# A new order of all pieces, and pad instructions ahead, in an attention and maxout-FFN kernel on one core

## The chip, the cores and the metric

One NeuronCore of a Trainium2 chip runs the whole program. The metric is device time in microseconds (us) of one execution, as a median over runs. Engines by the profile's names: PE is TensorE's matmul, PEld its weight load, DVE is VectorE, ACT is ScalarE, POOL is GpSimd, SP is SyncE.

## The reference

Eight batches of eight heads, 576 rows, head dimension 64, 32 memory slots; then a maxout feed-forward layer over all 4608 rows.

```python
def _attn_ref(q, k, v, phi):
    a = softmax(phi, axis=2)                       # over the sequence
    k_m = np.einsum('bhsm,bhsd->bhmd', a, k)
    v_m = np.einsum('bhsm,bhsd->bhmd', a, v)
    scores = (1/np.sqrt(64)) * np.matmul(q, k_m.transpose(0, 1, 3, 2))
    attn = softmax(scores, axis=-1)                # over the 32 slots
    return np.matmul(attn, v_m)

def _moe_ref(x, w1, w2, w3, w_out):                # x: 4608 x 512
    h = np.maximum(np.maximum(x @ w1, x @ w2), x @ w3)
    return h @ w_out                               # d_ff = 768
```

(The softmaxes are written out in the reference with maximum, exp and sum; they are shortened here.)

## The kernel before

The kernel never forms the attention output. Per batch it folds v_m into the weights, so that the feed-forward layer is applied to the attention weights themselves (256 of them per row instead of 512 columns). It uses max(a, b, c) = c + max(a - c, b - c, 0): w1 - w3 and w2 - w3 replace w1 and w2, and w3 goes with w_out into one small product.

The work is a list of pieces, written out by hand in one string (lines 810 to 838). A word such as `F8@2!` means piece F8 of batch 2; the mark ! swaps the engine that does the piece's copy or elementwise work. `issue` (line 769) calls the function of each letter, and every engine's instruction stream is the order of the list: nothing is rearranged afterwards. An engine takes its instructions in that order and stops at the first one whose inputs aren't ready. The letters:

- L0 to L3, J, H, h: loads of phi, k, v, q of a batch (J, H, h are parts), all issued by POOL except phi of batch 0 (SP); Y: the weights. q, k, v and the weights are turned from fp32 into bf16 on the way.
- E: exp of phi (ACT). B: the products with k and v (72 small matmuls, line 256), which from batch 2 on read a packed copy of k that r0 makes (POOL, or ACT with !). N: normalisation; K: transposes of the result (line 315); Q: transposes of q (DVE, line 330).
- S: scores and their exp (lines 351, 360). a, s, c, m, X: softmax by transposes on DVE (lines 410 to 450), m on POOL or, with !, on DVE. M, R and, in batches 0 and 1, part of X do it with ones-matmuls.
- W, O: products of w3 and w_out (lines 189, 197). V: w1 - w3 and w2 - w3 in four column ranges, on DVE or, with !, on POOL (line 218). In batch 0 the folds use w1, w2, w3 as they come, and V overwrites w1, w2 after that.
- D0 to D2 (and D4 in batch 0): the folded weights of a batch by columns, D3: the small product (line 462).
- F0 to F11: the hidden layer, even for the first operand, whose relu goes to ACT or, with !, DVE; odd for the second, whose max is always on DVE (line 526).
- t, T: the output product of batches 0 and 1 (lines 672, 690, 699, 708), where t is its first four matmuls; T4@7 is the last (lines 742, 753). U, A, P: the output product of batches 2 to 7 in Strassen-Winograd form: sums of weights (U, on POOL or DVE), of hidden rows (A), seven products (P, line 624).
- g: sends an output tile of batch 0 (ACT's queue, line 730). Other outputs are sent by SP.
- Z: matmuls on zeros in the first 20 us.

Results of PE lie in PSUM, eight banks that the digits of `banks` deal out in the order of the pieces; a digit is the bank, or the first of two. A piece can't start on a bank before the copy of the piece that had it is done. The output tile `ot` has four buffers, taken in turn:

```python
opool = ctx.enter_context(tc.tile_pool(name="opool", bufs=4))
...
ot = opool.tile([P, 2, DM], FP32, name="ot")[:, 0]
```

The four outputs of batch 0 stay in them until their g; T3@1 and T4@1 take the first two again. Inputs phi and q have two buffers each, k as loaded two, v and the packed k three.

Of the kernel before, what the change touches and what calls it, by code (L numbers as in the profile page):

```python
# [9 lines left out]
BF16 = mybir.dt.bfloat16  # L10
# [5 lines left out]
def kernel(  # L16
# [12 lines left out]
    nc = tc.nc  # L29

    B, H, S, D = q.shape
    M = phi.shape[-1]
    P = 128
# [11 lines left out]
    const = ctx.enter_context(tc.tile_pool(name="const", bufs=1))  # L45
# [18 lines left out]
    K1 = NP * NC * KS  # L64
# [20 lines left out]
    def load_ph(b):  # L85
        ph = inp.tile([P, NP, NC, M], FP32, name="ph", tag="ph")
        loaded.setdefault(b, {})["ph"] = ph
        dst = ph.rearrange("p j c m -> p j (c m)")
        if b == 0:
            for h in halves:  # L90
                nc.sync.dma_start(out=dst[:, h], in_=by_pair(phi, b)[:, h])
        else:
            nc.gpsimd.dma_start(out=dst, in_=by_pair(phi, b))

    def load_kv(b, i, h=slice(0, NP)):
        kv = vs[b % 3] if i else ks[b % 2]
        nc.gpsimd.dma_start(  # L97
            out=kv[:, h].rearrange("p j c d -> p j (c d)"),
            in_=by_pair((k, v)[i], b)[:, h],
        )  # L100

    def pack(b, swap):
        out_, in_ = krs[b % 3][:, :, :, 0:D], ks[b % 2]
        if swap:
            nc.scalar.copy(out=out_, in_=in_)
        else:
            nc.gpsimd.tensor_copy(out=out_, in_=in_)  # L107

    def load_q(b, h=slice(0, NP)):
        if "q" not in loaded.setdefault(b, {}):  # L110
            loaded[b]["q"] = inp.tile([P, NP, NC, D], BF16, name="qq", tag="qq")
        nc.gpsimd.dma_start(  # L112
            out=loaded[b]["q"][:, h].rearrange("p j c d -> p j (c d)"),
            in_=by_pair(q, b)[:, h],
        )

    def load_w(i):
        w = (moe_w1, moe_w2, moe_w3)[i]
        nc.gpsimd.dma_start(  # L119
            out=w_sb[:, :, i], in_=w.rearrange("(j p) f -> p j f", p=P)  # L120
        )
# [3 lines left out]
    def load_wo():  # L125
        nc.gpsimd.dma_start(out=wo_sb, in_=moe_w_out.rearrange("(t p) c -> p t c", p=P))
# [3 lines left out]
    warm = const.tile([P, BANK], BF16, name="warm")  # L130
# [7 lines left out]
    for i in range(P // M):  # L138
# [4 lines left out]
    banks = iter(  # L143
        "".join(
            """
            00232204420145545045026406426402640264023462467420742602462062460264024603604206
            42604620642164646240624607402604260240402402420724062042642024204204260424026427
            402742002442072420426045026520026265260602406243352
            """.split()
        )  # L150
    )
# [1 line left out]
    def one_bank():  # L153
        return psum[:, int(next(banks))]
# [5 lines left out]
    def warm_up(n):  # L160

        po = one_bank()
        for _ in range(n):
            nc.tensor.matmul(  # L164
                po[:, 0:BANK], lhsT=warm[:, 0:P], rhs=warm, start=True, stop=True
            )
# [46 lines left out]
    def w_diff(n, swap):  # L213

        c, end = [(0, BANK), (BANK, DF), (2 * BANK, 2 * DF), (DF, 2 * BANK)][n]
        while c < end:
            e = min(end, (c // DF + 1) * DF)
            (nc.gpsimd if swap else nc.vector).tensor_tensor(  # L218
                out=w12[:, :, c:e],
                in0=w12[:, :, c:e],  # L220
                in1=w_sb[:, :, 2, c % DF : c % DF + e - c],
                op=ALU.subtract,
            )
            c = e
# [202 lines left out]
    def att_rec(b, g):  # L427
        x = st[b]["ts"][:, groups(g)]
        nc.vector.reciprocal(out=x, in_=x)  # L429
# [302 lines left out]
    def ffn2_last(b, c0):  # L732
# [18 lines left out]
        for i, (c, po) in enumerate(zip(cs, pos)):  # L751
# [13 lines left out]
            else:  # L765
                nc.scalar.copy(out=ot[:, c], in_=po)
                nc.scalar.dma_start(out=rows, in_=ot[:, c])

    def issue(b, n, swap):

        i = int(n[1:]) if len(n) > 1 else None
        {
            "I": lambda: [make_identity(nc, ident)]
            + [nc.gpsimd.memset(x[:, :, :, D:], 1.0) for x in krs],
            "Y": lambda: load_w(i) if i < 3 else load_wo(),
            "L": lambda: load_ph(b) if i == 0 else load_q(b) if i == 3 else load_kv(b, i - 1),
            "J": lambda: load_q(b, halves[i]),
            "H": lambda: load_kv(b, i % 2, halves[i // 2]),
            "h": lambda: load_kv(b, 0, slice(i, i + 1)),
            "r": lambda: pack(b, swap),  # L780
            "E": lambda: [att_exp(b, h) for h in (halves if b == 0 else [slice(0, NP)])],
            "B": lambda: att_kv(b, i),
            "N": lambda: att_kv_norm(b, swap, i),
            "K": lambda: att_kv_t(b, swap, i),
            "Q": lambda: att_q(b, i),
            "S": lambda: att_score(b),
            "a": lambda: att_t(b, i),
            "s": lambda: att_sum(b, i),
            "c": lambda: att_rec(b, i),
            "m": lambda: att_mul(b, i, swap),  # L790
            "X": lambda: (ones_mul if (b, i) in ONES else att_back)(b, i),
            "M": lambda: ones_sum(b, i),
            "R": lambda: ones_rec(b, i),
            "D": lambda: fold(b, i, swap),
            "F": lambda: ffn1(b, i, swap),
            "T": lambda: ffn2(b, i, swap),
            "U": lambda: combine_w(b, i, swap),
            "A": lambda: combine_a(b, i, not swap),
            "P": lambda: products(b, i, swap),
            "W": lambda: w3_t(i, swap),  # L800
            "g": lambda: send(i),
            "d": lambda: fold_begin(i),
            "t": lambda: ffn2_begin(b, i),
            "O": lambda: w3_o(i, swap),
            "V": lambda: w_diff(i, swap),
            "Z": lambda: warm_up(i),
        }[n[0]]()


    for w in """  # L810
        E@0 h2@0 h3@0 h0@0 h1@0 L3@0 Z25@0 B0@0 Y2@0 I@0 N0@0 Z2@0 K0@0! Q0@0 Q1@0 Z9@0 S@0 Z2@0
        M0@0 M1@0 R0@0 R1@0 W0@0 Y3@0 W1@0 W2@0 Z6@0 O1@0 H3@0 O3@0 O2@0 H1@0 X1@0 B1@0
        X0@0 N1@0 K1@0 O0@0 Y0@0 D1@0! D0@0! D3@0 F10@0 F0@0! F8@0 Y1@0 L0@1 L1@1 J0@1
        F2@0! F6@0 V0@0! D4@0! D2@0 E@1 J1@1 F4@0! F1@0 F5@0 L2@1 F3@0 F7@0 F9@0 L3@2
        F11@0 B0@1 N0@1! t1@0 L1@2 t2@0 Q1@1 Q0@1 T2@0 K0@1! V1@0 V3@0 T1@0 S@1 L0@2
        B1@1 U0@9! N1@1! M1@1 a0@1 R1@1 t3@0 K1@1! T3@0 L2@2 s0@1 L1@3 c0@1 V2@0 D0@1
        D1@1! L0@3 D2@1 L2@3 t0@0 r0@2 X1@1 m0@1! X0@1 T0@0 F10@1! Q0@2 F6@1 E@2 F7@1
        F0@1 g2@0 F11@1 L3@3 F1@1 D3@1 Q1@2 F2@1 B@2 U1@9 F4@1 L1@4 L0@4 N@2 F3@1 F8@1
        K@2 g1@0 F5@1 L2@4 S@2 F9@1 D1@2! t3@1 E@3 D0@2 D2@2 D3@2 L3@4 a@2 T3@1 s@2 U3@9
        T4@1! c@2 m@2! r0@3 X@2 B@3 F0@2 U0@2 N@3 F8@2! F6@2 K@3 U1@2 Q0@3 L1@5 F2@2  # L820
        L0@5 Q1@3 U3@2 F10@2 g0@0 F3@2 F4@2 F9@2 F11@2 U2@9 S@3 a@3 s@3 t2@1 c@3 g3@0
        D3@3 D2@3 L2@5 U2@2 D0@3 U0@3 t0@1 r0@4! E@4 F1@2 T0@1! U1@3 F5@2 T2@1! F7@2
        t1@1 m@3 L3@5 A0@2! X@3 L0@6 T1@1! F6@3 F4@3! D1@3! B@4 N@4 L1@6 A1@2! F0@3 Q1@4
        F2@3 Q0@4 L2@6 A2@2! F8@3 K@4! F7@3 P1@2! F1@3 S@4 P2@2 F10@3 D0@4 a@4 D1@4!
        P0@2 A3@2! s@4 c@4 F3@3 P4@2 E@5 r0@5! F11@3 F9@3 m@4 F5@3 L3@6 P5@2 A0@3! T4@3!
        A1@3! D3@4 B@5 X@4 N@5 D2@4 Q1@5 Q0@5 P6@2 F2@4 K@5 P3@2 F10@4! S@5 L1@7 P1@3!
        D2@5 D1@5! a@5 F11@4 P2@3 F8@4 s@5 c@5 U2@3 L0@7 F4@4! F0@4 F6@4 r0@6! L2@7 P0@3
        F1@4 F7@4 F9@4 P4@3 E@6 A2@3! A3@3! F3@4 F5@4 P3@3 D0@5 m@5 L3@7 U3@3 D3@5 B@6
        A0@4! A1@4! X@5 N@6 P5@3 F6@5 F8@5! Q0@6 r0@7 F2@5 Q1@6 F10@5 K@6! F9@5 U0@5
        F4@5 F7@5 P6@3! S@6 E@7 F3@5 P1@4 a@6 F5@5 F11@5 P2@4 D0@6 U0@4 B@7 D3@6 U2@4  # L830
        N@7 s@6 P0@4 A2@4! F0@5 F1@5 Q1@7 K@7! U1@4 A3@4! P4@4 D1@6! A0@5! D1@7! c@6
        D2@7! m@6 P3@4! U3@4 P5@4! D0@7 D2@6 D3@7 U2@6 Q0@7 X@6 T4@5 S@7 A1@5! A3@5!
        P6@4! F10@6 a@7 F6@6 s@7 F4@6 F11@6 F0@6 F7@6 c@7 P1@5 P2@5 F2@6! U2@5 F5@6 F3@6
        P0@5 U1@5 F1@6 m@7 F8@6 A2@5! X@7 P4@5 P3@5 F4@7 U0@6 U1@6 F10@7 U3@5 F9@6 P5@5!
        F5@7 F8@7 A0@6! P1@6! A1@6! F2@7 F6@7 F0@7 P6@5! U0@7 F7@7 F3@7 F1@7 P2@6! F11@7
        F9@7 A0@7 P0@6 A2@6! A1@7 P4@6 A3@6 U3@6! P1@7 P2@7 A2@7 P5@6 P3@6 U2@7! U1@7
        P4@7 P0@7! A3@7 P6@6 U3@7! P5@7 P3@7! P6@7! T4@7!
    """.split():
        n, b = w.rstrip("!").split("@")
        issue(int(b), n, w.endswith("!"))  # L840


# [28 lines left out]
```

## Time and profile before

| | |
|---|---|
| time, median of 3 runs | 160.61 us (160.39 to 161.18) |
| the profiled execution | 160.76 us, of which the span is 159.0 us |
| busy in the span: PE | 149.6 us (94%), 2218 matmuls |
| PEld | 100.3 us (63%) |
| DVE | 116.8 us (73%) |
| ACT | 98.8 us (62%) |
| POOL | 109.2 us (69%) |
| granted TensorE clock | 0.999 |
| DMA queues, share of 16 engines' span | POOL's 70.2%, the two others for data 15.8% and 2.2% |

The span is the profiled time between the first and the last event of the execution; the rest of the 160.76 us lies around it. Times within the profile are counted from the span's start. A line of the timeline reads: start, duration, engine, line of the kernel, operation, output <- input, shapes, count, and in brackets the idle time before it and what ended it. A line of the windows by stage reads: the stretch and its length, then busy time and number of instructions of PE, PEld, DVE, ACT and POOL, granted clock, DMA share and GB/s. A line of the waits reads: engine, line and output, <- whom it waited for: us in total, times, longest.

### The profile page before, as it was taken

Reading aid. Unit: us, or ns where it says so; the run is one execution under the profiler, and the core shown is the slowest. Engines: PE = TensorE matmul, PEld = TensorE weight load, DVE = VectorE, ACT = ScalarE, POOL = GpSimd, SP = SyncE. Lnnn points to the kernel's source line nnn. Section 1 sums busy time; section 2 is a strip of 40 time slices with the busy share of each in tenths; the row PEclk is TensorE's granted clock in tenths of the full one; section 3 lists DMA queues with packets and bytes.
Section 4 is the critical chain, followed back from the end, with each engine's and each line's share of the span. In section 5 each row is a group of like instructions: output and inputs, shape, how many; then the busy total and the mean of one; then the engine's idle time right before and its main releaser. Section 6 shows DMA issues by size and latency. Waiting matters only on the chain.

```text
span 159.0 us, 5179 instructions
## 1 busy us (share of the span) xinstructions
PE 149.6 (94%) x2218; PEld 100.3 (63%) x2228; DVE 116.8 (73%) x203; ACT 98.8 (62%) x142; POOL 109.2 (69%) x101
## 2 busy tenths in 40 slices
PE   6987798999798999999999999999999999999992
PEld 2442443574456538556776768887774888888871
DVE  2022803698988899787989688999998895679871
ACT  3205335723888699799699878886788826424110
POOL 7961102995039948889999999799969997890000
PEclk9999999999999999999999999999999999999999
DMA  5999999999999999999999999999303500332554
GB/s 150 168 199 209 205 210 211 281 207 210 207 281 225 298 236 243 307 262 214 323 246 277 213 255 284 278 239 246 111 0 136 200 4 0 132 132 70 177 187 164
DMA packets 22934, 31.78 MB, mean 200 GB/s; under 512 B 1152, under 2 KB 18560, under 8 KB 22912
## 3 DMA queue, kind: packets, MB, share of 16 engines
q0 software_dynamic: 16128, 21.43, 70.2%
q1 hardware_dynamic: 6064, 8.85, 15.8%
q10 hardware_dynamic: 720, 1.18, 2.2%
q8 instruction: 17, 0.28, 0.7%
q14 instruction: 5, 0.04, 0.1%
HBM read 39.32 MB, written 9.44 MB: 307 GB/s over the span
## 4 chain that ended last, share of the span: by engine, by line
PE 72%; DMA 19%; POOL 5%; issue 1%; ACT 1%; POOLq 0%
PE psum L513 26%; PE psum L624 24%; DMA w_sb<-in_moe_w_dram 13%; DMA kvr<-in_v_dram 6%; PE psum L462 5%; PE psum L690 4%; PE psum L672 3%; PE psum L256 3%; PE psum L699 2%; PE psum L351 2%; POOL ko L97 1%; PE psum L708 1%; POOL qq L112 1%; POOL w_sb L119 1%; PE psum L753 1%
## 5 line engine op out<-in xcount | busy, mean ns | idle before, releaser
L513 PE MATMUL psum<-hx,wp 128*128 128x288 bf16 x384 | 53.7, 286 | 0.7 <-DVE wp L181 0.3
L513 PEld LDWEIGHTS <-wp 128*128 128x128 bf16 x384 | 36.6, 98 | 12.3 <-issue 1.5
L526 DVE TENSOR_TENSOR hx<-psum,h 128x576 bf16<-128x576 f32 x48 | 34.1, 744 | 3.3 <-PE psum L513 2.7
L177 ACT CAST wp<-psum 128x1024 bf16<-128x1024 f32 (+1 forms) x30 | 28.2, 993 | 2.7 <-PE psum L462 2.3
L175 ACT ACTIVATE h<-psum 128x576 bf16<-128x576 f32 x38 | 23.8, 651 | 8.9 <-PE psum L513 8.7
L624 PEld LDWEIGHTS <-hx 128*128 128x128 bf16 x192 | 18.4, 98 | 3.5 <-issue 0.9
L360 ACT ACTIVATE e<-psum 128x576 bf16<-128x576 f32 x16 | 9.5, 649 | 7.5 <-PE psum L351 7.5
L549 POOL TENSOR_TENSOR w_sb<-hx 128x1024 bf16<-128x1024 bf16 x5 | 10.6, 2130 | 4.0 <-DVE hx L526 2.6
L164 PE MATMUL psum<-warm 128*128 128x512 bf16 x42 | 11.8, 435 | 1.4 <-DVE warm L131 1.2
L330 DVE STREAM_TRANSPOSE qT<-qq 128x576 f32<-128x576 f32 x16 | 11.6, 757 | 2.0 <-DMA qq<-in_q_dram 2.0
L624 PEld LDWEIGHTS <-w_sb 128*128 128x128 bf16 x120 | 11.4, 98 | 2.5 <-issue 0.7
L107 POOL COPY kvr<-ko 128x2304 bf16<-128x2304 bf16 x3 | 6.3, 2108 | 7.7 <-DMA ko<-in_k_dram 7.7
L218 POOL TENSOR_TENSOR w_sb<-w_sb 128x2048 bf16<-128x2048 bf16 x1 | 4.1, 4065 | 10.4 <-PE psum L462 10.4
L436 POOL TENSOR_TENSOR t<-t,sm 128x1152 bf16<-128x1152 bf16 x5 | 10.6, 2127 | 0.6 <-DVE sm L429 0.5
L549 POOL TENSOR_TENSOR w_sb<-w_sb,hx 128x1024 bf16<-128x1024 bf16 x5 | 10.6, 2128 | 0.3
L234 ACT ACTIVATE e<-ph 128x1152 bf16<-128x1152 f32 (+1 forms) x9 | 9.6, 1063 | 1.8 <-DMA ph<-in_phi_dram 1.8
L549 POOL TENSOR_TENSOR hx<-hx 128x1024 bf16<-128x1024 bf16 x5 | 10.7, 2130 | 0.0
L549 POOL TENSOR_TENSOR twb<-wp 128x256 bf16<-128x256 bf16 x11 | 7.3, 670 | 3.9 <-ACT wp L177 3.9
L624 PE MATMUL psum<-w3T,hx 128*128 128x256 bf16 x72 | 9.8, 273 | 0.0
L624 PE MATMUL psum<-wo_sb,hx 128*128 128x256 bf16 x72 | 9.8, 273 | 0.0
L656 DVE TENSOR_TENSOR ot<-psum,snap 128x512 f32<-128x512 f32 x12 | 8.3, 689 | 1.9 <-PE psum L624 1.3
L97 POOL DMA_DIRECT2D ko<-in_k_dram x11 | 7.7, 700 | 2.9 <-DMA qq<-in_q_dram 1.5
(106 smaller groups left out, 272.2 us busy)
## 6 DMA issues: line engine op xcount, KB each, us to landing
out_dram<-ot SPq DMA_DIRECT2D x8, 512.0 KB, 4.2
qq<-in_q_dram POOLq DMA_DIRECT2D x7, 576.0 KB, 13.5
ph<-in_phi_dram POOLq DMA_DIRECT2D x7, 576.0 KB, 15.3
ko<-in_k_dram POOLq DMA_DIRECT2D x7, 576.0 KB, 16.1
kvr<-in_v_dram POOLq DMA_DIRECT2D x7, 576.0 KB, 18.0
out_dram<-ot SPq DMA_DIRECT2D x14, 256.0 KB, 2.2
w_sb<-in_moe_w_dram POOLq DMA_DIRECT2D x3, 768.0 KB, 17.9
out_dram<-ot ACTq DMA_DIRECT2D x4, 256.0 KB, 6.2
```

The source lines that it names most:

```text
L97: nc.gpsimd.dma_start(out=kv[:, h].rearrange("p j c d -> p j (c d)"), in_=by_pair((k, v)[i], b)[:, h],)
L164: nc.tensor.matmul(po[:, 0:BANK], lhsT=warm[:, 0:P], rhs=warm, start=True, stop=True)
L175: nc.scalar.activation(out=out_, in_=in_, func=AF.Relu)
L177: nc.scalar.copy(out=out_, in_=in_)
L234: nc.scalar.activation(out=s["e"][:, js], in_=loaded[b]["ph"][:, js], func=AF.Exp)
L330: nc.vector.transpose(out=s["qT"][:, j].rearrange("p j c r e -> p (j c r e)").bitcast(FP32), in_=loaded[b]["q"][:, j].rearrange("p j c d - ...
L360: nc.scalar.activation(out=e2[:, a].rearrange("p (t r c) -> p t r c", t=2, c=NC), in_=sc[a][:, :, 0:SH].rearrange("p t (c r) -> p t r c", ...
L436: (nc.vector if swap else nc.gpsimd).tensor_tensor(out=t, in0=t, in1=x.to_broadcast(list(t.shape)), op=ALU.mult,)
L513: nc.tensor.matmul(acc[:, h, 0:SH], lhsT=wps[b][:, g, w * DF + ft * P : w * DF + (ft + 1) * P], rhs=attn[:, g, c0 : c0 + SH], start=(g == ...
L526: nc.vector.tensor_tensor(out=hT[:, row(ft), (b % 2) * S : (b % 2 + 1) * S].rearrange("p (h n) -> p h n", h=2), in0=a, in1=s["h1", ft], op ...
L549: eng.tensor_tensor(out=out_, in0=in0, in1=in1, op=op)
L624: nc.tensor.matmul(po[:, q * CH : (q + 1) * CH], lhsT=lhs(k, q), rhs=rhs(k), start=(i < 3 and k == 0 and q == 0), stop=(k == KT and q == 1 ...
```

## The change

The list of pieces gets another order and, for 62 pieces, the other setting of the mark !; the set of pieces is the same. Up to F10@0 the order is as before. The banks are dealt out anew to fit. q of batch 2 (L3@2) is issued after k and v of that batch (L1@2, L2@2), not before. A new piece p makes n copies of a single column of the zero tile `warm` into a tile of two columns that nobody reads: 41 on DVE (p41@0!, first in the list), 8, 30 and 14 on ACT around E@0 and after K0@0. The diff, with the order cut after batch 3's first pieces:

```diff
+    pads = const.tile([P, 2], BF16, name="pads")
+
+    def pad(n, swap):
+
+        for i in range(n):
+            (nc.vector.tensor_copy if swap else nc.scalar.copy)(
+                out=pads[:, swap : swap + 1], in_=warm[:, 0:1]
+            )
...
+            "p": lambda: pad(i, int(swap)),
...
-        E@0 h2@0 h3@0 h0@0 h1@0 L3@0 Z25@0 B0@0 Y2@0 I@0 N0@0 Z2@0 K0@0! Q0@0 Q1@0 Z9@0 S@0 Z2@0
+        p41@0! p8@0 E@0 p30@0 h2@0 h3@0 h0@0 h1@0 L3@0 Z25@0 B0@0 Y2@0 I@0 N0@0 Z2@0 K0@0! p14@0 Q0@0 Q1@0 Z9@0 S@0 Z2@0
         M0@0 M1@0 R0@0 R1@0 W0@0 Y3@0 W1@0 W2@0 Z6@0 O1@0 H3@0 O3@0 O2@0 H1@0 X1@0 B1@0
-        X0@0 N1@0 K1@0 O0@0 Y0@0 D1@0! D0@0! D3@0 F10@0 F0@0! F8@0 Y1@0 L0@1 L1@1 J0@1
-        F2@0! F6@0 V0@0! D4@0! D2@0 E@1 J1@1 F4@0! F1@0 F5@0 L2@1 F3@0 F7@0 F9@0 L3@2
-        F11@0 B0@1 N0@1! t1@0 L1@2 t2@0 Q1@1 Q0@1 T2@0 K0@1! V1@0 V3@0 T1@0 S@1 L0@2
-        B1@1 U0@9! N1@1! M1@1 a0@1 R1@1 t3@0 K1@1! T3@0 L2@2 s0@1 L1@3 c0@1 V2@0 D0@1
-        D1@1! L0@3 D2@1 L2@3 t0@0 r0@2 X1@1 m0@1! X0@1 T0@0 F10@1! Q0@2 F6@1 E@2 F7@1
-        F0@1 g2@0 F11@1 L3@3 F1@1 D3@1 Q1@2 F2@1 B@2 U1@9 F4@1 L1@4 L0@4 N@2 F3@1 F8@1
-        K@2 g1@0 F5@1 L2@4 S@2 F9@1 D1@2! t3@1 E@3 D0@2 D2@2 D3@2 L3@4 a@2 T3@1 s@2 U3@9
-        T4@1! c@2 m@2! r0@3 X@2 B@3 F0@2 U0@2 N@3 F8@2! F6@2 K@3 U1@2 Q0@3 L1@5 F2@2
-        L0@5 Q1@3 U3@2 F10@2 g0@0 F3@2 F4@2 F9@2 F11@2 U2@9 S@3 a@3 s@3 t2@1 c@3 g3@0
+        X0@0 N1@0 K1@0 O0@0 Y0@0 D1@0! D0@0! D3@0 F10@0 F8@0 F0@0 F6@0! F4@0 Y1@0 D2@0!
+        D4@0 L0@1 L1@1 J1@1 F2@0 F1@0 F11@0 F3@0 F7@0 V1@0! F5@0 F9@0 E@1 B0@1 N0@1!
+        t0@0 t2@0 J0@1 Q1@1 t1@0 L2@1 Q0@1 K0@1! V2@0 L0@2 T2@0! S@1 V0@0 T1@0 a0@1 U0@9
+        B1@1 M1@1 V3@0! s0@1 N1@1! t3@0 c0@1 m0@1! K1@1 R1@1 T0@0! D1@1! X0@1 X1@1 D0@1!
+        T3@0! D2@1 E@2 F8@1! L1@2 F2@1! L2@2 F6@1 F3@1 L3@2 r0@2 F4@1 F5@1 D3@1 B@2 N@2!
+        F7@1 F10@1 Q0@2 F0@1 K@2! Q1@2 F9@1 F11@1 S@2 F1@1 D1@2! D2@2 t3@1 g2@0 g1@0
+        L1@3 a@2 U1@9 s@2 L0@3 L2@3 c@2 m@2! L3@3 L1@4 E@3 D3@2 D0@2 X@2 L0@4 T3@1 r0@3
+        T4@1 B@3 F10@2 F2@2 N@3 U2@2 F11@2 g0@0 F6@2 U0@2 F3@2 K@3! U1@2 F4@2 Q0@3 F0@2
+        U2@9 L2@4 Q1@3 L3@4 F8@2 g3@0 F5@2 F9@2 S@3 L0@5 L1@5 t2@1 L2@5 a@3 D0@3 D2@3
...
```

The swapped pieces that the prediction speaks of further on are r0@7 (from POOL to ACT) and A2@6 (from POOL to DVE).

More of the change, by code (lines that the diff above doesn't have):

```diff
@@ L145 @@
             """
-            00232204420145545045026406426402640264023462467420742602462062460264024603604206
-            42604620642164646240624607402604260240402402420724062042642024204204260424026427
-            402742002442072420426045026520026265260602406243352
+            00232204420145545045026402640640260426016724247642042604260426042604620461246042
+            60420642046214642640246042672406420462024024002460264026306463460460603464063460
+            264026404646020460260360404304640404026426436367372
             """.split()
@@ L821 @@
-        L0@5 Q1@3 U3@2 F10@2 g0@0 F3@2 F4@2 F9@2 F11@2 U2@9 S@3 a@3 s@3 t2@1 c@3 g3@0
[L822 to L837, printed above, removed]
+        X0@0 N1@0 K1@0 O0@0 Y0@0 D1@0! D0@0! D3@0 F10@0 F8@0 F0@0 F6@0! F4@0 Y1@0 D2@0!
@@ new lines @@
+        T4@1 B@3 F10@2 F2@2 N@3 U2@2 F11@2 g0@0 F6@2 U0@2 F3@2 K@3! U1@2 F4@2 Q0@3 F0@2
+        U2@9 L2@4 Q1@3 L3@4 F8@2 g3@0 F5@2 F9@2 S@3 L0@5 L1@5 t2@1 L2@5 a@3 D0@3 D2@3
+        r0@4! D3@3 E@4 s@3 U3@9 c@3 t1@1 m@3 F1@2 T1@1 F7@2 T2@1 L3@5 t0@1 A0@2! X@3
+        T0@1 F6@3! F7@3 F2@3 D1@3! L0@6 B@4 A2@2! N@4 F4@3 Q1@4 F0@3 F10@3 U3@2 A1@2!
+        F5@3 F8@3 Q0@4 K@4 P1@2 F9@3 S@4 L1@6 P2@2! a@4 D1@4! s@4 D0@4 A3@2! c@4 F1@3
+        m@4 U0@3 P4@2 F3@3 E@5 r0@5! P0@2 F11@3 U1@3 X@4 P5@2 T4@3! D3@4 B@5 D2@4 N@5
@@ new lines @@
+        L2@6 P6@2 F0@4 Q0@5 Q1@5 F8@4 K@5 P3@2! S@5 F6@4! F4@4 F2@4 a@5 F7@4 D2@5 D1@5!
+        s@5 F10@4 c@5 L3@6 P1@3 F3@4 E@6 P2@3! F9@4 r0@6! A0@3! F11@4 A1@3! F1@4 P4@3
+        L0@7 F5@4 A3@3! U2@3 P0@3 D0@5 B@6 m@5 X@5 L1@7 D3@5 A2@3! N@6 Q0@6 P3@3 F6@5
+        F0@5 Q1@6 A0@4! F4@5! P5@3 F10@5 F8@5! L2@7 K@6! F2@5! F5@5 U3@3 E@7 P6@3! S@6
+        F7@5 r0@7! a@6 P1@4 L3@7 F11@5 U2@4 U0@5 F9@5 A1@4! F1@5 U0@4 P2@4! D0@6 B@7
+        U1@4 A3@4! A2@4! U3@4 N@7! D3@6 s@6 P0@4! F3@5 K@7! P4@4 U2@5 c@6 D1@6! D2@7!
@@ new lines @@
+        Q1@7 D1@7! P3@4 P5@4 D2@6 Q0@7 D3@7! D0@7 T4@5! U0@6 S@7 P6@4 m@6 X@6 a@7 A0@5!
+        A1@5! F6@6 F8@6! U1@5 s@7 P1@5 F10@6 c@7 F2@6 P2@5! A2@5! m@7 F9@6 F11@6 F0@6
+        A3@5! P4@5! F1@6 F7@6 P0@5 U3@5 X@7 F4@6 F5@6 F3@6 P5@5 F8@7 F2@7 P3@5! F4@7
+        F5@7 A0@6! U1@6 U0@7 P6@5 A1@6! U2@6 F0@7! F6@7! F10@7 F1@7 F11@7 P1@6! F3@7
+        F9@7 U2@7 P2@6 F7@7 A2@6 P4@6 A3@6 U1@7 A0@7 U3@6! P0@6 A1@7 P1@7 P5@6 P3@6 P2@7
+        A2@7 A3@7 P4@7 P6@6 U3@7! P0@7 P5@7! P3@7! P6@7! T4@7!
```

## Prediction

> **What bounds it now.** I read the page first, then windows by stage, TensorE's (PE) timeline from 25 to 62 us, the queues' landings, and the waits.
>
> ```profile
> 0.00:25.00 25.00, 20.85 (x268) 9.85 (x272) 6.80 (x23) 8.60 (x13) 10.63 (x23) 1.00 1.07 191
> 25.00:60.00 35.00, 33.10 (x624) 18.58 (x627) 29.12 (x46) 24.70 (x39) 21.82 (x19) 1.00 1.18 240
> 60.00:150.00 90.00, 89.79 (x1294) 67.25 (x1288) 76.84 (x129) 64.50 (x90) 76.75 (x59) 1.00 0.76 187
> 150.00:159.00 9.00, 5.89 (x55) 4.58 (x53) 3.99 (x7) 1.01 (x3) 0.00 (x0) 0.99 0.56 193
> ```
>
> The windows (first column after the length: PE busy) say where a new order can act. From 60 to 150 us PE lacks 0.21 of 90 us. Both orders hold the same pieces, so PE's work there is the same, and only a new stall can change that stage. The end is 12 products and T4 back to back, then a store. The first 25 us keep their order. What is left is 25 to 60, where PE lacks 1.9 us, and the timeline shows some of it:
>
> ```profile
> 27.21 0.66 PE L513 MATMUL psum<-hx,wp 128*128 128x288 bf16 x4
> 28.17 2.13 PE L513 MATMUL psum<-hx,wp 128*128 128x288 bf16 x16 [0.30 <-DVE wp L181]
> ...
> 49.73 0.65 PE L513 MATMUL psum<-hx,wp 128*128 128x288 bf16 x4 [0.23 <-DVE hx L526]
> 50.59 0.80 PE L256 MATMUL psum<-kvr,e 64*32 64x130 bf16 x72 [0.21 <-ACT wp L177]
> ...
> 53.67 0.48 PE L351 MATMUL psum<-qT,kvt 32*32 32x288 bf16 x32
> ```
>
> ```profile
> PE psum L256 <- DMA kvr<-in_v_dram: 0.8, 1, 0.8
> ```
>
> F10 to F0 of batch 0 start 0.96 apart where an F piece takes 0.49; B1@1 waits 0.77 for v of batch 1. The last fence is a line of the waits between 25 and 62 us. Loads bound this stage as much as PE: asked issue by issue, POOL's queue lands in order of issue, v1 at 40.53 (31.68 + 8.85), then q2 43.43, k2 46.27, ph2 47.82, v2 50.46, k3 54.09, ph3 55.64, v3 59.08. So q takes 2.90, k 2.84, ph 1.55, v 2.64.
>
> **The change, step by step.** The sum goes against the profiled run's own 160.76 us (span 159.0 and 1.76 around it), 0.15 over the median 160.61.
>
> *Batch 0's first products (27 to 35 us).* F8 now comes before F0, and F8's columns are D1's, which ScalarE (ACT) has copied at 27.15. F10, F8, F0 run at 27.2, 27.7, 28.2: the 0.47 hole closes. F6 and F4 follow to 29.65. D2 needs w2, which lands at 30.04 (8.77 + 21.28) in either order: 0.4 given back. D4 ends near 30.8, then seven F of 0.49 with 0.05 of wait for D4's copy: B0@1 starts near 34.4 (before: 34.93; k1 lands at 34.26).
>
> *V on POOL.* V0, 4.07 us and behind a wait of 10.4, becomes V1 and V3, 2.1 each by half the columns, and U0@9, 1.65. Behind V1 in POOL's queue stand J0@1 and the loads after it: J0@1 issues near 28.6 instead of 30.95, V3 runs to 34.6, then k2, v2, q2 by 36.9. The queue is still working off earlier issues until 36.28, so no load becomes late or early by this: v1 lands at 40.53 again. VectorE (DVE) gives up V1, V3 and U0@9 (0.6 each) and takes V0 (1.16).
>
> *Up to B1@1.* t0 (0.87) is now done before it. B0@1 34.4, t0 35.1, t2, t1, K0, T2, S@1 38.9, T1 end at 40.2; B1@1 waits for v1 as before, 40.58. The gain there is t0's 0.87. T3, T0, D0 to D2 of batch 1 then run without the old gaps but wait for copies; I get the first F of batch 1 at 45.4 against 46.06: 0.66 ahead.
>
> *q of batch 2 behind v.* With the durations above: ph2 42.1, k2 44.9, v2 47.6, q2 50.46. B@2 needs POOL's copy of k (44.9 + 2.1 = 47.0) and v2. It starts near 48.8 with six F done (before 50.59 with seven): 1.3 ahead. Q0@2 now waits for q2 at 50.46, and the F copies of DVE queue behind it: Q0, Q1 end at 52.15, S@2 starts at 52.3 against 53.67, both with 11 F done. So 1.37 ahead.
>
> *The stores g2 and g1.* Here the gain goes. The output tile has four buffers; T3@1 and T4@1 take those of T2@0 and T1@0, so they wait until g2 and g1 have landed. Before, ACT issued these at 48.2 and 53.0. Now both stand on ACT behind the copies of D1@2 and D2@2, that is, behind S@2.
>
> ```profile
> L730 ACTq DMA_DIRECT2D out_dram<-ot x4: 338/338/374, 48.2 to 65.7; - x4
> DMA to landing us min/median/max: 5.8/6.2/6.5
> ```
>
> ```profile
> 59.99 1.13 ACT L177 COPY ot<-psum 128x512 f32<-128x512 f32 x2
> ```
>
> The first fence is the answer for the stores' line, the second ACT's timeline. g1 landed at 53.01 + 5.82 = 58.83, 1.6 before T4@1's copy at 60.47. From S@2's start in the new order: first exp done 1.25 (0.58 to its start, 0.65, as at 53.67), D1 and D2 on PE 0.6, issue of g2 and g1 0.4, landing 6.2, T4@1's copy (now DVE) 0.75: 9.2. F11@2, the third F of batch 2, takes the banks of T3@1 and T4@1, so it starts at 52.3 + 9.2 = 61.5. Without the wait it would be 60.35 (t3, D3, D0, T3 and T4 at their old lengths put B@3 at 58.55, then B 0.8 and two F). The third F of batch 2 started at 61.35 before (60.38 + 2 x 0.49). Equal PE work, 0.15 later. N@3 on DVE stands behind T4@1's wait and K@3, F3@2 behind N@3; I get S@3 at 65.7 with ten F done against 65.04 with nine, 0.17 late. v3 lands at 57.5 to 59.1 (without the two stores that shared 53 to 59, or as before), so B@3 is not the last wait.
>
> *POOL's queue past r0@2.* r0@2 now stands ahead of batch 3's loads. POOL waits there for k2 (44.9), packs to 47.0, issues k3 (before: 36.0), spends 1.65 on U1@9, then issues ph3 and v3 at 49.5 and 50.2. The queue works on q2 until 50.46 and the quickest load in the trace landed 4.0 after its issue (the first k, 1.25 to 5.22), so k3 can land at 53.3 and v3 isn't held. Were v3 late by 2.5 us or more, B@3 would be the last wait instead of the stores.
>
> *The rest of the order, from 65 us.* By pieces times the rows' durations, from S@3 on DVE and POOL keep their load within 0.5 us (A2@6 goes from POOL, 2.1, to DVE, 0.6) and ACT gains 1.9 (r0@7, 2.1). In 60 to 150 these engines are idle for 13, 25 and 13 us, and the least distance between a bank's copy and its next use is about 0.9 us of PE work in both orders. Cost 0; without that cover, a single held copy is 0.3 to 0.6.
>
> *Pads.* 41 on DVE, 8, 30 and 14 on ACT; no instruction so small stands in the trace. Bounds: 0.01 (the one-column MEMSETs, 3 in 0.08 us) and 0.25 (ACT's 128-column COPY). I take 0.14: two 576-column exps start 0.54 apart, 1024-column CASTs 0.90, which leaves 0.08 fixed, and the 1152-column exp from SBUF adds 0.06. Their cover is in ACT's and DVE's waits:
>
> ```profile
> 3.71 0.68 ACT L234 ACTIVATE e<-ph 128x576 bf16<-128x576 f32 x1 [1.68 <-DMA ph<-in_phi_dram]
> 10.71 0.37 ACT L177 COPY kvt<-psum 128x256 bf16<-128x256 bf16 x1 [5.47 <-PE psum L315]
> 13.56 1.19 ACT L360 ACTIVATE e<-psum 128x576 bf16<-128x576 f32 x2 [2.47 <-PE psum L351]
> 9.52 0.17 DVE L276 RECIPROCAL rden<-psum 128x2 f32<-128x2 f32 x1 [7.61 <-PE psum L256]
> ```
>
> 8, 30, 14 and 41 times 0.14 are 1.1, 4.2, 2.0 and 5.7: all fit, cost 0. What the pads are to avoid I don't find: ACT's three CASTs from 57.29 and DVE's copies near 50 run without a gap that PE doesn't explain. Gain 0. [...]
>
> Sum: 160.76 + 0.15 = 160.91 for a profiled run, 160.8 as a median.
>
> **Rivals.**
> *The head start survives.* If g1 lands within 5.0 us, T4@1's copy isn't held, F11@2 starts at 60.35, 1.0 earlier than the third F before: 159.6. For it: stores in the last 12 us of the span land in 2.2. Against: those have the queues to themselves, while the four of ACT needed 5.8 to 6.5 with POOL's loads running, which they still do near 55. [...] Chance 0.25, also for other gains there.
> *Slower: head start lost, hold kept.* Decided at S@2. If Q0@2's wait for q2 or a late copy puts S@2 where it was, 53.67, the 9.2 us behind it put F11@2 at 62.87, 1.5 late: 162.1. For it: one late copy anywhere in 27 to 52 is enough, and q2 is now the last load. Against: v2 and k2 are 2.9 and 1.4 earlier. 0.16.
> *Pads overrun.* At 0.25 each, 52 pads leave ACT about 3.3 late at S@0's exp, of which 1.35 of waits absorb: 2 us, 162.7. 0.05.
> *The order does nothing*: 160.6, 0.04.
>
> **The numbers.** The hold, 0.50, has its own range from 160.4 (q2-bound S@2 at 52.1) to 161.9. About 0.10 of it is over 0.8 late. 0.5%, 0.8 us, is about what a measurement of this kernel tells from no change. Faster 0.25; same 0.40 + 0.04 = 0.44; slower 0.10 + 0.16 + 0.05 = 0.31. The range 159.4 to 162.1 leaves out little of the first rival and the far side of the others.
>
> **What would show it.** Right: g2 and g1 issued on ACT near 54.2, landing near 60.5; PE idle over 1 us before the third F of batch 2, put down to a DVE or ACT copy of ot; B1@1 still at 40.6; S@2 near 52.3. Wrong: no such gap, or S@2 not earlier; pads ending after 10.7 on ACT; PE idle past 65 us, which I have at none.

## The result, and the profile after

The changed kernel takes 165.57 us (median of 4 runs, 165.16 to 167.69) against 160.53 us: a ratio of 1.030, 95% interval 1.0265 to 1.0334. It is slower, by 5.0 us. (The run of 167.69 had a lower clock, 0.969; such runs count in the medians but not in the ratios, here and below.) The profiled execution is one of 165.16 us, with a span of 163.0 (before: 160.76 and 159.0). So 4.0 us were lost inside the span and 0.4 outside it.

The windows by stage, with the columns explained with the profile before, answer to the four lines shown there:

```profile
0.00:25.00 25.00, 21.55 (x255) 10.83 (x257) 12.89 (x62) 18.02 (x65) 10.63 (x23) 0.93 1.07 189
25.00:60.00 35.00, 33.79 (x679) 19.03 (x670) 27.98 (x41) 26.37 (x44) 21.63 (x20) 1.00 1.16 224
60.00:150.00 90.00, 87.34 (x1242) 64.17 (x1230) 74.53 (x121) 64.04 (x90) 75.15 (x60) 0.98 0.80 190
150.00:163.00 13.00, 9.97 (x93) 8.25 (x90) 6.95 (x13) 2.71 (x5) 0.00 (x0) 0.99 0.47 161
```

From 25 to 60 us the new order is denser, as meant: 33.79 us of PE against 33.10. But the first 25 us ran at a granted clock of 0.93 instead of 1.00, and the stretch from 60 to 150, where PE lacked 0.21 us before, now lacks 2.66 and has a clock of 0.98. PE's timeline, from 28 to 67 us, shows where:

```profile
28.40 2.62 PE L513 MATMUL psum<-hx,wp 128*128 128x288 bf16 x20
...
41.55 0.75 PE L256 MATMUL psum<-kvr,e 64*32 64x64 bf16 x72
...
49.51 0.83 PE L256 MATMUL psum<-kvr,e 64*32 64x130 bf16 x72
...
53.21 0.49 PE L351 MATMUL psum<-qT,kvt 32*32 32x288 bf16 x32
...
60.13 1.15 PE L513 MATMUL psum<-hx,wp 128*128 128x288 bf16 x8
62.31 0.28 PE L513 MATMUL psum<-hx,wp 128*128 128x288 bf16 x1 [1.02 <-ACT ot L177]
64.00 2.80 PE L513 MATMUL psum<-hx,wp 128*128 128x288 bf16 x11 [1.41 <-DVE ot L181]
```

The holes of before are closed: batch 0's first five F pieces run without a gap (28.40), and B1@1 (41.55) no longer waits for v. B@2 (49.51, with one F fewer ahead of it) and S@2 (53.21) are 1.08 and 0.46 earlier than before. Then two F of batch 2 run, and the third stands for T3@1's copy and again for T4@1's. The answer for the stores' line, and the lines of ACT and of DVE that take the two output tiles, name what those copies wait for:

```profile
L730 ACTq DMA_DIRECT2D out_dram<-ot x4: 338/356/450, 55.2 to 68.7; - x4
DMA to landing us min/median/max: 6.4/6.9/7.6
```

```profile
55.20 0.86 ACTq L730 DMA_DIRECT2D out_dram<-ot  x2
...
61.67 0.58 ACT L177 COPY ot<-psum 128x512 f32<-128x512 f32 x1 [1.89 <-DMA out_dram<-ot]
```

```profile
63.26 0.69 DVE L181 COPY ot<-psum 128x512 f32<-128x512 f32 x1 [3.29 <-DMA out_dram<-ot]
```

g2 and g1 are issued at 55.20 and 55.61 and land at 61.59 and 63.17. The third F gets its second bank at 64.00. Before, three F ran without a stop from 60.36, the third from 61.35:

```profile
60.36 1.65 PE L513 MATMUL psum<-hx,wp 128*128 128x288 bf16 x12
...
65.04 0.48 PE L351 MATMUL psum<-qT,kvt 32*32 32x288 bf16 x32
```

S@3 starts at 69.53 with ten F of batch 2 done (65.04 with nine before, so 4.0 behind after 0.49 for the piece more): all of the span's loss is there by then, and PE is full behind it in both kernels.

The lead is the other place. ACT's and DVE's timelines, and PE's, from 2 to 20 us:

```profile
5.06 6.75 ACT L774 COPY pads<-warm 128x1 bf16<-128x1 bf16 x30
11.71 0.36 ACT L177 COPY kvt<-psum 128x256 bf16<-128x256 bf16 x1
11.97 3.14 ACT L774 COPY pads<-warm 128x1 bf16<-128x1 bf16 x14
15.02 1.18 ACT L360 ACTIVATE e<-psum 128x576 bf16<-128x576 f32 x2
```

```profile
1.93 7.80 DVE L774 COPY pads<-warm 128x1 bf16<-128x1 bf16 x41
9.72 0.17 DVE L276 RECIPROCAL rden<-psum 128x2 f32<-128x2 f32 x1
```

```profile
15.71 1.18 PE L372 MATMUL psum<-e,blkones 128*128 128x288 bf16 x4 [1.60 <-ACT e L360]
16.68 2.75 PE L189 MATMUL psum<-ident,w_sb 128*128 128x128 bf16 x24
```

The same two lines of PE before:

```profile
14.26 0.94 PE L372 MATMUL psum<-e,blkones 128*128 128x288 bf16 x4 [0.23 <-ACT e L360]
15.61 1.51 PE L189 MATMUL psum<-ident,w_sb 128*128 128x128 bf16 x24 [0.40 <-DMA w_sb<-in_moe_w_dram]
```

A pad takes ACT 0.22 us (3.14 / 14) and DVE 0.19 (7.80 / 41). ACT's copy of K0 comes 1.0 later than before, its exp of S@0 1.5 later, and PE stands 1.60 for it where it stood 0.23. The W products behind it (L189) then take 2.75 us instead of 1.51. The windows ahead of that place and at it, and around the stores' wait, say why (after the length: PE, PEld, DVE, ACT, POOL busy, then the clock):

```profile
12.45:15.86 3.41, 1.77 (x38) 0.62 (x37) 0.59 (x1) 3.06 (x14) 0.16 (x1) 1.00 1.18 208
15.86:19.27 3.41, 3.39 (x28) 2.92 (x28) 1.33 (x2) 3.00 (x5) 0.70 (x1) 0.50 1.24 209
60.24:63.65 3.41, 1.33 (x9) 0.79 (x9) 0.39 (x1) 1.68 (x3) 3.33 (x5) 1.00 1.18 255
63.65:67.06 3.41, 3.06 (x15) 2.04 (x15) 2.09 (x7) 0.65 (x1) 3.41 (x5) 0.50 1.11 313
```

The granted clock fell to 0.50 from 15.86 to 19.27 us and from 63.65 to 67.06, for 3.41 us each time. The two starts lie 47.79 us apart, 14 times 3.41; from this I read windows of 3.41 us, one behind the other. In the windows just ahead PE was busy 1.77 and 1.33 us, shares of 0.52 and 0.39. The first half clock costs W 1.24; the second makes the eleven F matmuls behind the hold take 2.80, where the same eleven at full clock take 1.51 (in the run with ten pads and the hold, below).

### The profile page after: what moved, and what is told of

The parts are those of the page before. It is cut to its first block, busy times and chain, and to the rows that moved or that the text cites. A ratio compares the mean times of both kernels' runs of the same rounds, so it can differ in the third digit from the quotient of the medians.

```text
span 163.0 us, 5266 instructions
## 1 busy us (share of the span) xinstructions
PE 152.7 (94%) x2217; PEld 102.3 (63%) x2228; DVE 122.3 (75%) x236; ACT 111.1 (68%) x203; POOL 107.4 (66%) x102
## 4 chain that ended last, share of the span: by engine, by line
PE 78%; ACT 11%; DMA 7%; issue 2%; DVE 1%; SPq 0%; ACTq 0%; DVEq 0%
PE psum L513 27%; PE psum L624 23%; ACT pads L774 5%; DMA out_dram<-ot 5%; PE psum L462 5%; PE psum L672 4%; PE psum L690 4%; PE psum L197 3%; PE psum L256 3%; DMA ph<-in_phi_dram 2%; PE psum L699 2%; PE psum L351 2%; PE psum L189 2%; ACT wp L177 2%; ACT e L360 1%
## 5 line engine op out<-in xcount | busy, mean ns | idle before, releaser
L513 PE MATMUL psum<-hx,wp 128*128 128x288 bf16 x384 | 55.2, 291 | 2.6 <-DVE ot L181 1.4
L175 ACT ACTIVATE h<-psum 128x576 bf16<-128x576 f32 x37 | 22.7, 658 | 10.1 <-PE psum L513 10.0
L177 ACT CAST wp<-psum 128x1024 bf16<-128x1024 f32 (+1 forms) x28 | 27.1, 1003 | 2.4 <-PE psum L462 2.2
L638 ACT COPY snap<-psum 128x512 f32<-128x512 f32 x10 | 5.9, 595 | 8.8 <-PE psum L624 8.8
L774 ACT COPY pads<-warm 128x1 bf16<-128x1 bf16 x52 | 10.1, 195 | 1.6
L218 POOL TENSOR_TENSOR w_sb<-w_sb 128x1024 bf16<-128x1024 bf16 x2 | 4.3, 2126 | 10.5 <-PE psum L462 10.5
L549 POOL TENSOR_TENSOR twb<-wp 128x256 bf16<-128x256 bf16 x12 | 7.9, 674 | 3.1 <-ACT wp L177 3.1
L179 DVE TENSOR_SCALAR h<-psum 128x576 bf16<-128x576 f32 x11 | 8.0, 748 | 2.5 <-PE psum L513 2.4
## 6 DMA issues: line engine op xcount, KB each, us to landing
w_sb<-in_moe_w_dram POOLq DMA_DIRECT2D x3, 768.0 KB, 18.6
```

The source lines that it names most:

```text
L175: nc.scalar.activation(out=out_, in_=in_, func=AF.Relu)
L513: nc.tensor.matmul(acc[:, h, 0:SH], lhsT=wps[b][:, g, w * DF + ft * P : w * DF + (ft + 1) * P], rhs=attn[:, g, c0 : c0 + SH], start=(g == ...
L549: eng.tensor_tensor(out=out_, in0=in0, in1=in1, op=op)
L774: (nc.vector.tensor_copy if swap else nc.scalar.copy)(out=pads[:, swap : swap + 1], in_=warm[:, 0:1])
```

## Experiments

Two questions were open: how much of the loss is the wait for g2 and g1 (the hold), and what the pads do. The first runs went out with the view that the pads only cost time. From their surprise came two theories about the packets of the queue that the page lists as "q14 instruction" (5 packets, 0.04 MB, so 8 KB each). I took each for the fetch of a block of ACT's instructions, which no run shows. A: ACT stops wherever such a block ends; and B: only a store issue of ACT that meets the fetch of its next block is slow.

| kernel | median us | ratio to before (95%) |
|---|---|---|
| new order, no pads | 169.94 | 1.057 (1.052 to 1.062) |
| old order with the pads | 161.09 | 1.003 (0.999 to 1.006) |
| new order, pads, no hold | 161.59 | 1.004 (1.001 to 1.007) |
| new order, no pads, no hold | 164.66 | 1.017 (1.010 to 1.023) |
| no pads, early stores | 161.27 | 1.003 (1.001 to 1.005) |
| old order, late stores | 162.49 | 1.012 (1.010 to 1.013) |
| ten pads, no hold | 160.76 | 1.001 (0.999 to 1.003) |
| pads, early stores | 161.35 | 1.005 (1.002 to 1.009) |
| old order, late stores, two pads | 167.72 | 1.043 (1.036 to 1.051) |
| four pads, no hold | 161.43 | 1.002 (0.999 to 1.005) |
| ten pads, with hold | 162.91 | 1.016 (1.010 to 1.021) |
| after with more zeros | 163.80 | 1.017 (1.013 to 1.022) |
| old order, late stores, one pad | 167.74 | none (two runs) |
| old order, late stores, three pads | 167.26 | 1.042 (1.026 to 1.058) |

**The order without its pads.** `p41 p8 p30 p14` leave the list of after.

```
-        p41@0! p8@0 E@0 p30@0 h2@0 ... K0@0! p14@0 Q0@0
+        E@0 h2@0 ... K0@0! Q0@0
```

> The new order without the 93 pads. Theory (two separate costs, pads in the lead and the wait for the stores g2 and g1, each followed by 3.4 us at half clock): the first F of batch 0 is back at 27.2 us, no half clock near 15 us, S@2 starts near 52.2, g2 and g1 are issued near 54.3, the third F of batch 2 still waits for g1 and starts between 61.8 and 63, and the half clock after it may or may not stay: 161.5 to 163.5 us. Rival 1 (the pads' lateness is the only cause, and the stores' wait follows from it): 159.5 to 160.5. Rival 2 (the new order itself is worse): over 164.

It got slower still, by over 4 us against after, far outside the range of the theory; that was the surprise of the study. ACT's timeline:

```profile
54.33 1.01 ACT L177 CAST wp<-psum 128x1024 bf16<-128x1024 f32 x1
54.71 5.14 ACTq L730 DMA_DIRECT2D out_dram<-ot  x1
55.23 1.02 ACT L177 CAST wp<-psum 128x1024 bf16<-128x1024 f32 x1
59.87 0.46 ACTq L730 DMA_DIRECT2D out_dram<-ot  x1
60.38 1.16 ACT L234 ACTIVATE e<-ph 128x1152 bf16<-128x1152 f32 x1 [4.12 <-issue]
```

The issue of g2, 0.37 us in before, takes 5.14, and nothing behind it on ACT can start. The exp of phi of batch 3 is late, B@3 waits 2.78 for it, g1 goes out at 59.87, and PE stands another 2.61 and 1.43 for the two output tiles. In the trace an 8 KB packet of the instruction queue (q14) starts at 58.30, inside that issue. The two such packets of the first 60 us come at 50.5 and 58.2 in before and at 18.6 and 23.1 in after: with the pads they fall into the lead. The trace doesn't say for which engine a packet of q14 is; that the one at 58.30 is ACT's is inferred from the long issue around it.

**The pads alone, in the old order.** The same `p` words in before's list.

> The order of before with the same 93 pads in the same places. Theory: ACT's pads take 0.22 us each, S@0's exp is 1.4 us late, PE waits 1.6 us before M0 and runs at half clock from 15.5 to 18.9 us; the first F of batch 0 starts 1.2 late, of which v of batch 1 (0.77 of wait in the kernel before) takes some back: 161.0 to 162.0 us. Rival 1 (the pads explain the whole loss): 164.5 to 166. Rival 2 (pads cost nothing): 160.5.

No difference that can be measured. The old order has no store issue near the packet (58.2 in before, with issues at 53.0 and 63.3), so there was nothing for the pads to gain, and the lead's later waits hide them when the clock stays full, as it did in the profiled run (granted clock 0.999, PE 0.55 busy in the window with the wait).

**The hold taken away.** Batches 0 and 1 put two outputs into one tile of `ot`, so that T3@1 and T4@1 find a free one.

```
-        ot = opool.tile([P, 2, DM], FP32, name="ot")[:, 0]
+        if b > 1 or not spare:
+            x = opool.tile([P, 2, DM], FP32, name="ot")
+            spare[:] = [x[:, 0], x[:, 1]]
+        ot = spare.pop(0)
```

> The new order with pads; the output pieces of batches 0 and 1 share a buffer two by two (each uses one half), so T3@1 and T4@1 get a buffer that no store of batch 0 holds. Theory: no wait before the third F of batch 2, which starts near 61.1, no half clock after 60 us, only the pads' loss stays: 160.5 to 161.5 us. Rival 1 (the stores' wait hides another one, banks or X@2): PE still stops over 1 us near 61, 163 or more. Rival 2 (pads are the sole cause): 165.

161.59, some 4 us less than after with the same pads, and 0.1 above the range: the stores' wait and what it drags along is most of the loss. Nothing on PE waits for `ot` any more, and its clock was full throughout in the profile (1.000). PE stood 1.24 for the late exp in the lead, yet the first F of batch 0 started at 27.24 (27.21 before) and B1@1 still waited 0.55 for v: with a full clock the pads' lateness is absorbed there.

**Both taken away** (no hold, no pads).

> Both taken away: no pads, and the shared buffers. Theory: the head start that the prediction's first rival gave, the third F of batch 2 near 60.3 and no half clock: 159.2 to 160.0 us, faster than before. Rival (the new order itself is worse): 161 or more.

164.66, far from the range of the theory: g2's issue is long again (5.27 at 54.61, packet at 58.33), with nobody waiting for g2's tile. So the long issue harms by what stands behind it on ACT, and the two troubles are separate.

**The stores early, without pads.** g2 goes behind E@2 and g1 ahead of N@2, as early as in the old order.

```
-        T3@0! D2@1 E@2 F8@1! ... B@2 N@2!
-        ... D1@2! D2@2 t3@1 g2@0 g1@0
+        T3@0! D2@1 E@2 g2@0 F8@1! ... B@2 g1@0 N@2!
+        ... D1@2! D2@2 t3@1
```

> The new order without pads, with g2 sent after E@2 and g1 before N@2 (some 9 and 5 us earlier than in the run without pads), buffers as they were. Theory B (what the pads avoid is that ACT's issue of a store meets the fetch of its next instruction block, which lands near 58.3 us without pads: g2 took 5.1 us to issue there): no ACT gap near 56 to 60, no wait for a buffer, third F of batch 2 near 60.3, no half clock: 159.2 to 160.2 us, faster than before. Theory A (ACT stands still for 4 us at the end of its block whatever instruction stands there): a gap of about 4 us on ACT near 55 to 60 as in the run without pads, 163 to 165 us.

No long issue (0.38 and 0.34), no hold, and yet no gain: 161.27. On ACT no idle time from 40 to 66 us is longer than 1.51, and that one waits for phi of batch 3 (57.78), which speaks against A. But here B@3 waits 1.76 for v of batch 3 (PE, 60.60). Early stores run beside the loads that POOL issued, and v came late; that the stores caused it is argued, not shown.

**The stores late, in the old order.** g2 and g1 of before go behind t3@1.

```
-        F0@1 g2@0 F11@1 ... K@2 g1@0 F5@1 ... t3@1 E@3
+        F0@1 F11@1 ... K@2 F5@1 ... t3@1 g2@0 g1@0 E@3
```

> The order of before, no pads, with g2 and g1 moved behind t3@1 as in the new order. Theory B: g2's issue near 55 us meets ACT's fetch and takes about 5 us, ACT idle 4 us, PE stops before B@3 and again for T3@1 and T4@1's buffers: 167 to 171 us. Theory A, or the stores' wait alone: g2 and g1 issue in 0.4 us each, T4@1's copy waits until about 62, the third F of batch 2 near 63, half clock once: 162.5 to 165 us.

162.49: only the hold, 1.9 us. The issues took 0.38 and 0.34 and the packet started after them, at 59.67. The long issue that theory B foresaw did not come; the next runs show that the place was missed by one instruction.

**Ten pads, no hold.** Of all pads only ten, on ACT behind K0; shared tiles.

> The new order with the shared buffers and only ten pads on ACT (after K0@0, where 14 stood), none on DVE. [...] Theory B: g2's issue is short (under 1 us) or at most 1 us late, the lead is untouched (10 x 0.22 in a pause of 2.47), third F of batch 2 near 60.5: 159.3 to 160.5 us. Theory A: ACT's gap of 4 us only moves ahead to about 50, over 162 us. Rival C (it is DVE's pads that matter): as without pads, 163 to 166.

160.76, level with before. Issues of 0.37 and 0.46, and no idle time on ACT over 0.69 from 40 to 66 us, where A put a gap of 4 near 50: A has fallen. So has rival C, as there were no pads on DVE. The median is 0.3 above the range of B. The profiled execution is the fastest of all that were profiled, 160.07 with a span of 158.3, and has the new order's gain: S@3 starts at 64.81 with ten F done (65.04 with nine before), 0.7 ahead, just the span's gain. Over the runs no difference to before is left (ratio 1.001).

**The stores early, with all pads.**

> The changed kernel with its 93 pads, only g2 and g1 sent early as in the run without pads. Theory: no buffer wait, no half clock near 62 us; the lead stays about 1.2 us late: 160.4 to 161.6 us. If the move of the stores costs the loads that B@2 and B@3 wait for (k, v of batch 2 and 3 land 0.8 later for each store), up to 162.

161.35, as expected. In the profiled run (granted clock 0.989) PE waited 2.42 in the lead for the exp, and W behind it took 2.76, as at half clock in after; the hold and the long issue were gone, and so was most of the loss.

**The place of the store, to one instruction.** ACT's own list, counted with its instructions that only wait, has g2 at number 66 where the issue was long, and at 64 in the old order with late stores. Pads shift that by one each:

```
-        K0@0! Q0@0
+        K0@0! p2@0 Q0@0
```

> The order of before with g2 and g1 behind t3 of batch 1 (162.49 when run without pads) and two pads on ACT behind K0, so that the first store is ACT's 66th instruction, as it was where its issue took 5.1 us, instead of the 64th, where it took 0.38. Theory B (a store issue on ACT that comes at or right after the instruction at which ACT asks for its next block of code takes until that block has come): the first issue takes 4 to 5.5 us, the exp of phi behind it starts near 60.5, and the time is 166 to 169 us. Rival D (the long issue belongs to the new order, to its loads and its load on the queues, not to the place in the stream): issue 0.4 us, 162.3 to 162.8.

Two copies of one column, 0.4 us in the lead, cost 5.2 us:

```profile
55.15 4.37 ACTq L730 DMA_DIRECT2D out_dram<-ot  x1
55.30 1.02 ACT L177 CAST wp<-psum 128x1024 bf16<-128x1024 f32 x1
59.56 0.45 ACTq L730 DMA_DIRECT2D out_dram<-ot  x1
60.06 1.16 ACT L234 ACTIVATE e<-ph 128x1152 bf16<-128x1152 f32 x1 [3.73 <-issue]
```

Rival D has fallen: the new order isn't needed for the long issue. With one pad (stores 65th and 66th) and with three (67th and 68th):

> As the run with two pads, with one: the two stores are ACT's 65th and 66th instructions. Theory B (a store issue on ACT that comes at or behind the 66th instruction, where the next block is asked for, waits until it has come): the first issue takes 0.4 us, the second 4 to 5 us; the exp behind it again starts near 60, time 166 to 168.5. If the place weren't what counts: both issues under 0.7 us, 162.3 to 162.8.

> With three pads: the 66th instruction is the CAST of a folded weight, the stores are the 67th and 68th, right behind it. Theory B (the store waits for the outstanding block): the first issue takes 4 to 5 us, 166 to 168.5. Variant B' (only an issue that is itself the 66th): both under 0.7 us, 162.3 to 163.0.

In both the first store is the long one: 4.37 us as the 65th, 4.15 as the 67th; the second takes 0.45. So it need not be the 66th itself (B' has fallen), and my count was off by at least one: with one pad the second store was to be the long one. In all five long cases the q14 packet starts 1.53 to 1.55 us before the issue ends (57.98 and 59.53 in the fence's run). A lag as constant as that speaks for theory B, by which the issue waits for the packet. Why the stores at 64 and 65 escape is open: with them the packet started 3.4 us after the second issue.

**Four pads, no hold** (stores 70th and 71st).

> The order of after with shared output tiles, so without the store hold, and only four pads, on ACT behind K0. ACT's 66th instruction is then an exp of S of batch 2, near 53 us, and the stores are the 70th and 71st, 1 to 1.5 us behind it. Theory B (any store issue waits while the block asked for is under way): the first issue takes 3 to 4.5 us, ACT stands 2.5 to 3.5 us, time 163 to 164.5. Variant B' (only an issue that is itself the first instruction of the block is slow): issues 0.37 and 0.45 us, no gap, 160.5 to 161.0, as with ten pads (160.76).

Issues of 0.37 and 0.45, 161.43. But the last packet ahead of them started at 51.7, 2.4 us before the first issue, so none started inside them and the run doesn't tell B from B'; the run with three pads did. The 66th instruction started only at 53.32, after that packet, so the count gives the neighbourhood of the place and not the instruction itself. The median is 0.4 above the range of B'.

**The hold by itself** (after with ten pads on ACT).

> The changed kernel with ten pads on ACT instead of 52 and none on DVE: the output tiles are taken as in after, so T3 and T4 of batch 1 wait for the two stores, but ACT isn't late in the lead and no issue is long. This prices the store hold by itself in the new order. Theory: S of batch 2 near 52.6, the stores issued near 54.7 and 55.1, g1 landing near 62.5, the third F of batch 2 near 63.3 (61.35 before): 2 us, and 1.4 more if PE's idle time there halves the clock for one window: 162.6 to 164.4. Rival (the pads' lateness in the lead is the main loss): 160.8 to 161.5.

162.91, some 2.2 above the same without the hold. PE:

```profile
52.11 0.49 PE L351 MATMUL psum<-qT,kvt 32*32 32x288 bf16 x32 [0.16 <-ACT kvt L177]
...
61.65 0.28 PE L513 MATMUL psum<-hx,wp 128*128 128x288 bf16 x1 [0.77 <-ACT ot L177]
63.15 1.51 PE L513 MATMUL psum<-hx,wp 128*128 128x288 bf16 x11 [1.22 <-DVE ot L181]
```

S@2 comes at 52.11, the stores at 54.09 and 54.50 land at 60.93 and 62.31, and the third F has its second bank at 63.15, 0.15 from what was expected. PE's idle time is split between two windows (0.59 and 0.64 busy) and the clock stays full (1.000). In one of the other three runs (164.16) the clock was 0.989: it seems that the idle time falls on the windows differently from run to run.

**The clock.** After with `Z6` instead of `Z2` behind S@0, 1.5 us of matmuls on zeros in PE's wait.

> The changed kernel with six matmuls on zeros instead of two behind S of batch 0, in PE's wait for ACT's late exp. Theory: the half clock at 15.9 to 19.3 us came from PE's idle time just before (0.52 busy in 3.41 us); with 0.9 us of it filled, the clock stays full there, W takes 1.5 us again, the first F of batch 0 starts near 27.7 instead of 28.4; the store hold stays: 164.2 to 165.0 us. Rival (later waits for loads absorb the lead): the clock is full there, the time stays 165.2 to 165.9.

Three runs at a clock of 1.0 took 163.11, 163.58 and 164.02, on average 1.9 us less than the three of after at 0.978 (165.16, 165.21, 165.93); the two half-clock windows had cost PE 1.24 and 1.29 there. That is below the range expected, since the second window had gone too, which the zeros don't explain. There is no profile of these three runs, so whether the zeros or another phase of the windows kept the clock up is open.

## Why the prediction was wrong

It said 160.8 us, 159.4 to 162.1, with slower at 0.31.

**Up to S@2 it was right.** The run with ten pads, where ACT isn't late, has the order as forecast: B1@1 at 40.45 (forecast 40.6), B@2 48.40 (48.8), S@2 52.11 (52.3). The head start was there and went where the prediction put it, into T3@1's and T4@1's wait for g2 and g1. In the same order without the hold the profiled run kept 0.7 of it to S@3, though the median of that kernel shows no gain.

**The step that failed first is the size of the hold.** The sum had 9.2 us from S@2 to the third F; the run with ten pads has 11.04 (52.11 to 63.15), after 10.79 (53.21 to 64.00). The landing was taken as 6.2 from stores issued 2.4 us or more apart. Here g1 follows g2 by 0.41, and in every run with such a pair the second landed in 7.6 to 8.5 us, 1.0 to 1.2 more than the first (7.6 after 6.4 in after, 7.81 after 6.84 with ten pads and the hold). The first landed in 6.4 to 7.5 itself, often more than the 5.8 to 6.5 of before; why is open. A price for stores close together stood in the trace of before: three of 256 KB that SP issued from 73.32, less than 0.5 apart, landed in 7.04, 7.95 and 9.09. With 0.72 between them (old order, late stores) the two landed in 5.73 and 6.50. The issues made another 0.15. So the hold alone gave 162.91, not 160.8: above the range.

**Second, the pads' lateness.** 0.14 was taken; 0.22 was measured on ACT, close to the bound of 0.25 at which the rival gave 162.7. The 30 pads ended at 11.8 on ACT, past the 10.7 that the prediction had named as a sign of being wrong. The rival let 1.35 of waits absorb an overrun: in before PE waits 0.40 for w3 (L189) and 0.95 for w_out (L197). With a full clock they did absorb it (the run without the hold, 161.59, where L197 starts at 19.40; before 19.36). In after W itself ran at half clock, the cover of 0.95 before w_out was gone, and S@2 came 0.9 later than forecast.

**Third, a term that the sum didn't have: the clock.** Each of the two idle times was followed by 3.41 us at half clock (0.50), one in the lead and one behind the hold. In the lead 1.60 us of one wait, in a window with 1.64 idle in all, was enough. A wait of 1.83 that fell across two windows (the pads alone, granted clock 0.999) cost no clock.

The terms close: third F at 64.00 against 61.5 is 0.91 (S@2 late) + 0.15 + 1.36 (landing) + 0.08 = 2.5, and 1.3 of half clock behind it gives 3.8 at S@3 (69.53 against 65.7). The kernels, set side by side, say the same: 160.76 with ten pads and no hold, 162.91 with the hold, 163.1 to 164.0 with all pads and zeros at full clock, 165.2 to 165.9 with the two windows at half clock.

**"Gain 0" for the pads was wrong in kind.** In this order they save over 4 us with the hold (169.94 to 165.57) and some 2 us without it (by the ratios, 1.017 against 1.004). The prediction looked for a gap on ACT and DVE in before and found none, rightly; but before has no store issue at that place, and the change moves two stores there. The prediction followed the data of the two stores to their landing, but gave their issue 0.4 us wherever it stands in ACT's stream; without pads it takes 5.14 there. How few pads are enough, and that none is needed on DVE, the runs with ten and four show. The first run's expectation, that the pads only cost time, fell with it.

**The rivals.** Of the prediction's, "pads overrun" (0.05) came true together with the forecast hold, and their sum was worse than either. "The head start survives" needed a landing within 5.0 us; the second store took 7.6. Of the head start at S@2, 1.37 by the forecast, 0.46 was left: the rival of a lost head start came near, but through the pads and not through q2 (landed at 50.42, as forecast) or a late copy.

## What to carry to other kernels

In after PE lacked 1.64 and 2.08 us in a window of 3.41, and the half clock that followed cost 1.24 and 1.29 us more than the waits; with ten pads and the hold, 0.59 and 0.64 busy in two windows cost nothing more. So price an idle time together with PE's busy share around it. A store's landing taken from stores 2.4 us or more apart (6.2) was too short for a pair issued 0.41 apart (7.6): look in the trace for stores as close as those that the change will make. And where a kernel's DMA is issued by a compute engine, find where the packets of the instruction queue (q14 here) fall in the trace: moving the issue by one or two instructions cost some 5 us (162.49 against 167.74 and 167.72), and ten pads were enough where 93 had been put.

## What the runs showed of the hardware

- A store issue on ACT with an 8 KB packet of the instruction queue (q14) starting inside it took 4.15 to 5.27 us instead of 0.34 to 0.63, and ended 1.53 to 1.55 us after the packet's start (five runs: the new order without pads, with the hold and without; the old order with late stores and one, two or three pads). That it waits for the packet is the reading that fits all five. In before the packets at 50.47 and 58.22, with other work of ACT around them, left no gap on ACT that isn't put down to PE.
- In after, windows of 3.41 us at full clock with PE busy 0.52 and 0.39 were each followed by 3.41 us at a clock of 0.50. With 0.51 (no pads, early stores), 0.55 (the pads alone), and 0.59 and 0.64 (ten pads, with hold) the clock stayed full. So 1.64 us of idle time in a window were enough once, and about as much another time was not.
- Of two 256 KB stores issued 0.41 us apart on ACT's queue, with loads running, the second landed 1.0 to 1.2 us slower than the first, in 7.6 to 8.5 us (7.6 in after, 7.81 with ten pads and the hold).
- Copies of one column take ACT 0.22 us and DVE 0.19.
